# The opening of an attention and MLP kernel: first loads on other queues, shared roots, transposes twice, and a new order list

## The chip, the cores and the metric

The kernel runs on one core of a Trainium2 chip. The metric is the device time of one execution in microseconds; lower is better. The profile shows the engines PE (matrix multiplication; PEld is its weight load), DVE, ACT, POOL and SP. SP, ACT and POOL issue DMA transfers.

## The reference, cut to what matters

```python
def rmsnorm(x, g):
    rms = np.sqrt(np.mean(x * x, axis=-1, keepdims=True) + 1e-06)
    return x / rms * g
q_n, k_n = (rmsnorm(q, g_q), rmsnorm(k, g_k))      # q, k, v: (8, 12, 448, 64)
scores = 1.0 / np.sqrt(64) * np.matmul(q_n, k_n.transpose(0, 1, 3, 2))
attn = softmax(scores)                             # over the last axis
x = np.matmul(attn, v)                             # heads joined: (8, 448, 768)
xn = (x - mu) / np.sqrt(var + 1e-06) * g_ln        # layer norm over 768
out = x + np.maximum(xn @ w_ch1, 0.0) @ w_ch2      # 768 -> 3072 -> 768
```

There are eight batches, each with twelve heads of 448 rows of 64. All inputs and the output are 32-bit.

## The kernel before

Heads are worked on in pairs, six pairs a batch. The 448 rows of a head are 384 main rows, three to a partition, and 64 left rows; the left rows of a pair's two heads lie in the upper and the lower 64 partitions, so each is loaded by a DMA of its own. For each pair the kernel squares, sums and takes the root of queries and keys, scales them, splits the keys into a high and a low 16-bit part, transposes both on PE, multiplies (scores), exponentiates on ACT, multiplies by the values, and then does layer norm and the MLP for the batch.

Batch 0 is cut finely, since nothing is there to overlap with at the start. Its loads are issued by `load_first`. Its work and that of batch 1 stand as names in one list written out by hand, `ORDER`, which `first_attention` walks from front to back. Each name emits the instructions of one step; each engine runs its own instructions strictly in that order and waits by semaphores for the others. The dictionary `ENGINE` says which engine (A for ACT, V for DVE, P for POOL) does a step, where it is not the usual one. After the list, batches 2 to 7 follow a planner that is the same in both kernels.

The names, for key unit u (unit 0 and 1 are pairs 0 and 1, unit 2 and 3 two pairs each):

- `a` square, `d` sum, `h` root (two ACT instructions, Ln and Exp), `n` scale, `j` cast to the high part, `k` subtract for the low part; then `K` transposes a pair's keys on PE into the one bank `tr`, and `C` copies them out (`moved`).
- Queries come in five parts, `0.0`, `0.2`, `1.0`, `2.0`, `2.4`: third of the main rows, and first pair. `qa` square, `qt` sum, `qg` root, `qG` times the weights, `ql` scale, `qm` double (copy the 64 columns beside themselves), `Q` transposes on PE (`turn`), `QC` copies out (`keep`). The tiles `qn` that the parts are scaled into are two buffers in turn.
- `S` scores, `E` exponential, `V` values, `O` division into x, `T` and `A` statistics, `N` and `X` layer norm and its transposes, `XC` their copy, `U` and `R` the first MLP product of batch 0 and its ReLU. `S0.1.0` is query third 0, pair 1, first half. Two banks serve the scores.
- `L4k` loads the keys of unit 4 (batch 1), `z`, `za`, `zb` bring the values to 16 bits on POOL, `W0` and `W1` issue weights from POOL once the keys of unit 4 have landed, `G2` scales the layer norm's weights on POOL, `sp1`, `spm`, `sp2` multiply and spread the two weight vectors g.
- `F23` is 23 filler matmuls of the identity (L824), whose result nobody reads.
- Names without a dot and with a number from 4 on (`c4`, `j4`, `m4`) are the same steps for the units of batch 1.

Of the kernel before, what the change touches and what calls it, by code (L numbers as in the profile page):

```python
# [40 lines left out]
S1.1.1 O0.1 T0.0 qm2.0 qg2.4 E1.1.1 T0.1 S1.2.0 Q2.2 E1.2.0 S1.2.1 E1.2.1 A0 qG2.4 Q2.0 L5k
S1.3.0 V1.1 S1.3.1 ql2.4 E1.3.0 E1.3.1 qm2.4 S1.4.0 E1.4.0 V1.2 N0 S1.4.1 O1.0 QC2.0 X0 S1.5.0
V1.3 QC2.2 E1.4.1 S1.5.1 XC0 E1.5.0 T1.0 Q2.4 V1.4 S2.0.0 E1.5.1 V1.5 S2.0.1 O1.1 QC2.4 L5v
U0.0 E2.0.0 S2.0.2 E2.0.1 S2.1.0 b4 a4 c4 U0.1 E2.0.2 E2.1.0 R0.0 S2.1.1 T1.1 S2.1.2 V2.0 A1 d4
E2.1.1 S2.2.0 i4 N1 E2.1.2 X1 S2.2.1 E2.2.0 j4 V2.1 L5q S2.2.2 E2.2.1 e4 g4 E2.2.2 b5 a5 R0.1
S2.3.0 U0.2 E2.3.0 W2 S2.3.1 S2.3.2 XC1 U1.0 E2.3.2 E2.3.1 S2.4.0 c5 l4 k4 m4 S2.4.1 v4 E2.4.0
i5 E2.4.1 K6 d5 V2.2 S2.4.2 R1.0 C6 S2.5.0 e5 E2.4.2 Q6 V2.3 E2.5.0 D6 S2.5.1 za4 E2.5.1 S2.5.2
E2.5.2 R0.2 V2.4 K7 V2.5 S6.0 S6.1 E6.0 U1.1 O2.0 g5 S6.2 v5 zb4 O2.1 E6.1 U0.3 V6.0 S6.3 j5
E6.2 za5 l5 C7 k5 L6k L6v T2.0 R0.3 U1.2 v6 batch1 R1.1 T2.1 E6.3 za6 L6q S6.4 A2 S6.5 E6.4 zb5
Q7 b6 a6 U1.3 N2 W3 m5 S6.6 V6.1 D7 L7k d6 U1.4 c6 zb6 E6.6 V6.2 E6.5 i6 X2 S7.0 e6 XC2 R1.2  # L50
# [68 lines left out]
class _Fast:  # L119
# [353 lines left out]
    def first_pieces(self):  # L473
# [20 lines left out]

        def root(c):
            nc.scalar.activation(c["rt"], c["ssq"], AFT.Ln, scale=1.0 / D, bias=1e-6)
# [8 lines left out]
        def total(c):
            nc.vector.tensor_reduce(out=c["ssq"], in_=c["sq"], axis=AX.X, op=ALU.add)

        def key_unit(u, p0, m):
# [14 lines left out]
            def low():  # L523
                nc.vector.tensor_tensor(out=c["n"][:, :, 1], in0=k, in1=c["n"][:, :, 0],
                                        op=ALU.subtract)
# [13 lines left out]
        def query_part(ph, p0, p1):  # L539
# [10 lines left out]
            def square():  # L550
                start(c, g, "qn")
                for y, a in zip(src, at):
                    nc.scalar.activation(pair(c["sq"])[:, :, a], y, AFT.Square)
# [15 lines left out]
            def double():  # L569
                _on(nc, f"qm{tag}", "V").tensor_copy(out=c["n"][:, :, 1], in_=c["n"][:, :, 0])  # L570
# [4 lines left out]

            def turn(a, b):
                c["ps", a] = ps = self.ps_m.tile([128, 1024], FP16, tag="mlp", name="psQ")
                y = ps[:, 0:w * (b - a)].rearrange("p (w e s) -> p w e s", e=2, s=w // 2)
                last = n * (b - a) - 1
                for i in range(last + 1):  # L580
                    q, k = divmod(i, n)
                    out = y[:, q, :, 128:192] if k == 2 else y[:, q, k, 0:128]
                    nc.tensor.matmul(out, c["n"][:, n * (a - p0) + i], sh.id16, is_transpose=True,
                                     start=(i == 0), stop=(i == last))

# [724 lines left out]
```

## Time and profile before

| what | value |
|---|---|
| median of three runs | 600.67 us (599.64 to 603.43) |
| profiled execution | 598.46 us, of which the span is 596.8 us |
| PE busy | 580.5 us |
| ACT, DVE, POOL busy | 353.0, 292.7, 189.9 us |
| DMA | 75.25 MB, 126 GB/s on average |

Busy time is summed over the span. The prediction reads the first 60 us in more detail, where PE, DVE and ACT share the work otherwise than later. In rows of groups, the numbers after the first bar are the busy time in us and the mean of one in ns, and after the second the idle time just before and what ended it. In rows of the timeline, the first number is the start and the second the length in us.

### The profile page before, as it was taken

To read this page: it belongs to the slowest core of one execution; us is meant where nothing else is said; L and a number is where in the kernel's file an instruction comes from. 1 tells how busy PE (TensorE), PEld (TensorE's weight loads), DVE (VectorE), ACT (ScalarE), POOL (GpSimd) and SP (SyncE) were. 2 spreads that over 40 slices of the span, in tenths; PEclk is the share of its full clock that TensorE was granted. 3 is DMA by queue.
4 is the path that set the end of the run, shared out by engine and by line. 5 is a ranking of instruction groups with operands and counts; after the bars stand their busy time and mean duration, and the time that the engine had idled before them with its cause. 6 is when DMAs were issued, how large, how long until landed. Compare 5 with 4: busy or idle time off the path is not lost.

```text
span 596.8 us, 12445 instructions
## 1 busy us (share of the span) xinstructions
PE 580.5 (97%) x4989; PEld 361.9 (61%) x4989; DVE 292.7 (49%) x638; ACT 353.0 (59%) x671; POOL 189.9 (32%) x254
## 2 busy tenths in 40 slices
PE   5899999999999999999999999999999999999997
PEld 4889976545565666555566666654566666654565
DVE  6899778444455256724256255724256322440011
ACT  5987784379752897358843598538755387114300
POOL 3769330044650555132541345423512000000000
PEclk9999999999999999999999999999999999999999
DMA  8999998546975776946956496839723320040011
GB/s 268 209 249 203 220 240 186 118 147 106 153 156 134 137 128 128 171 131 73 154 134 140 76 142 145 184 110 124 135 61 88 82 63 1 27 106 1 1 53 57
DMA packets 130225, 75.25 MB, mean 126 GB/s; under 512 B 96468, under 2 KB 120356, under 8 KB 130164
## 3 DMA queue, kind: packets, MB, share of 16 engines
q1 hardware_dynamic: 113636, 44.92, 37.8%
q0 software_dynamic: 16128, 29.27, 23.2%
q8 instruction: 40, 0.66, 0.5%
q10 hardware_dynamic: 400, 0.23, 0.1%
q14 instruction: 21, 0.17, 0.1%
HBM read 52.30 MB, written 11.01 MB: 106 GB/s over the span
## 4 chain that ended last, share of the span: by engine, by line
PE 89%; DMA 4%; SPq 2%; ACT 1%; DVE 1%; POOL 1%; issue 1%; ACTq 0%; POOLq 0%
PE psC L1032 36%; PE psH L998 32%; PE psS L385 8%; PE oA L443 5%; PE psU L695 3%; DMA qkv<-in_v_dram 2%; PE oB L445 2%; PE psS L391 1%; SPq L172 1%; DMA w<-in_k_dram 1%; DMA hT<-in_k_dram 1%; SPq L164 0%; PE tr L353 0%; PE tr L336 0%; POOL gln L832 0%
## 5 line engine op out<-in xcount | busy, mean ns | idle before, releaser
L1032 PE MATMUL psC<-w,hT 128*128 128x384 f16 (+1 forms) x1368 | 235.5, 323 | 0.0
L998 PE MATMUL psH<-xnT,w 128*128 128x512 f16 (+1 forms) x1008 | 217.7, 356 | 0.0
L406 ACT ACTIVATE E<-psS,rr_all 128x448 f16<-128x448 f32 x273 | 171.5, 637 | 60.8 <-PE psS L385 59.3
L1032 PEld LDWEIGHTS <-hT 128*128 128x128 f16 x1368 | 127.1, 98 | 78.4 <-issue 3.9
L1000 ACT ACTIVATE hT<-psH 128x512 f16<-128x512 f32 (+1 forms) x168 | 93.8, 559 | 119.5 <-PE psH L998 117.7
L998 PEld LDWEIGHTS <-w 128*128 128x128 f16 x1008 | 91.1, 98 | 77.7 <-issue 3.0
L385 PE MATMUL psS<-qU,kU 128*128 128x448 f16 x252 | 86.4, 352 | 0.7 <-ACT E L406 0.6
L443 PEld LDWEIGHTS <-E 128*128 128x128 f16 x819 | 56.1, 98 | 35.9 <-issue 1.8
L265 POOL TENSOR_TENSOR qkv<-qkv,gprod 128x896 f32<-128x896 f32 x20 | 41.6, 2081 | 92.4 <-ACT khl L114 71.6
L1039 DVE SCALAR_TENSOR_TENSOR x<-psC,rs_all,x 128x384 f32<-128x384 f32 x48 | 29.3, 616 | 80.7 <-PE psC L1032 80.3
L443 PE MATMUL oA<-v,E 128*128 128x65 f16 x756 | 58.1, 193 | 0.1
L164 POOL DMA_DIRECT2D qkv<-in_k_dram x14 | 11.2, 798 | 122.8 <-ACT E L406 68.2
L456 DVE RECIPROCAL rec_all<-oA 128x6 f32<-128x6 f32 x42 | 8.2, 196 | 83.3 <-PE oA L443 82.8
L445 PE MATMUL oB<-v,E 128*128 128x65 f16 x252 | 45.3, 193 | 0.1
L257 DVE TENSOR_REDUCE ssq<-khl 128x14 f32<-128x896 f32 x21 | 22.7, 1081 | 45.6 <-ACT khl L114 45.5
L385 PEld LDWEIGHTS <-kU 128*128 128x128 f16 x252 | 24.3, 98 | 16.8
L257 DVE TENSOR_REDUCE ssq<-qn 128x14 f32<-128x896 f32 x21 | 22.8, 1084 | 22.1 <-ACT qn L114 22.1
L89 DVE SCALAR_TENSOR_TENSOR qn<-qkv,rr_all 128x256 f16<-128x256 f32 (+2 forms) x71 | 25.3, 416 | 17.0 <-ACT rr_all L261 16.9
L695 PE MATMUL psU<-xnT,w 128*128 128x128 f16 x432 | 27.1, 219 | 0.0
L445 PEld LDWEIGHTS <-E 128*128 128x128 f16 x273 | 26.3, 96 | 0.2 <-DVE xl L463 0.2
L695 PEld LDWEIGHTS <-w 128*128 128x128 f16 x432 | 25.2, 98 | 1.5 <-issue 0.4
L458 DVE TENSOR_TENSOR x<-oA,rec_all 128x384 f32<-128x384 f32 x42 | 23.4, 558 | 1.3
(158 smaller groups left out, 599.5 us busy)
## 6 DMA issues: line engine op xcount, KB each, us to landing
out_dram<-x SPq DMA_DIRECT2D x20, 384.0 KB, 2.5
qkv<-in_v_dram POOLq DMA_DIRECT2D x15, 384.0 KB, 7.2
qkv<-in_k_dram POOLq DMA_DIRECT2D x14, 384.0 KB, 3.9
qkv<-in_q_dram POOLq DMA_DIRECT2D x14, 384.0 KB, 5.4
w<-in_moe_w_ch_dram POOLq DMA_DIRECT2D x3, 1536.0 KB, 12.8
w<-in_moe_w_ch_dram POOLq DMA_DIRECT2D x2, 2304.0 KB, 20.9
qkv<-in_q_dram SPq DMA_DIRECT2D x7, 384.0 KB, 9.7
qkv<-in_v_dram SPq DMA_DIRECT2D x6, 384.0 KB, 8.1
```

Of the source, the lines that this page charges most:

```text
L89: nc.vector.scalar_tensor_tensor(out=out, in0=x, scalar=8.0, in1=r.unsqueeze(2).broadcast_to([x.shape[0], g, D]), op0=ALU.mult, op1=ALU.mult)
L257: nc.vector.tensor_reduce(out=c["ssq"][:, n], in_=c["sq", n], axis=AX.X, op=ALU.add)
L265: _on(nc, f"i{u}", "P").tensor_tensor(out=self.loads[u][1], in0=self.loads[u][1], in1=sh.gprod.unsqueeze(1).broadcast_to([128, g, D]), op= ...
L385: nc.tensor.matmul(ps[0][:, 0:S], c["main"][:, ts(i, 128)], c["q"][:, ts(h, S)], start=True, stop=True)
L406: self.nc.scalar.activation(out=o, in_=c.pop(("ps", i))[:, 0:S], func=AFT.Exp, scale=self.units[u][3][:, g:g + 1], bias=EXP_BIAS)
L443: nc.tensor.matmul(oA[:, t, cs], E[:, ts(t, 128)], rhs, start=(i == 0 and t == 0), stop=(i == 6 and t == 2))
L445: nc.tensor.matmul(oB[:, cs], E[:, 320:448], rhs, start=(i == 0), stop=(i == 6))
L695: nc.tensor.matmul(ps[:, ts(f, 128)], sh.w1[:, dc, ts(4 * k + f, 128)], self.xnT[:, dc, ts(t, 128)], start=(f == 0 and dc == 0), stop=(f = ...
L998: nc.tensor.matmul(ps[:, 0:N], sh.w1[:, dc, ts(f, 128)], xnT[:, dc, 0:N], start=(dc == 0), stop=(dc == NDC - 1))
L1000: nc.scalar.activation(out=hT[:, f, 0:N], in_=ps[:, 0:N], func=AFT.Relu)
L1032: nc.tensor.matmul(self.psC[:, 0:g[1]], self.hT[:, f, ts(t, 128)], sh.w2[:, h, f, c:c + g[1]], start=(f == 0), stop=(f == NFF - 1))
L1039: self.nc.vector.scalar_tensor_tensor(out=x, in0=self.sums.pop((b, t, g[0]))[:, 0:g[1]], scalar=self.rs[:, b, t:t + 1], in1=x, op0=ALU.mul ...
```

## The change

- The second left row of the first pair's keys is issued by SP, as its second DMA, instead of by ACT. The two weight vectors g are issued by ACT instead of by SP. The first query transfer comes after the second pair's keys, the identity is built after all of these.
- Roots are taken for two parts at once, where `ROOTS` says so: `h1` for key unit 1 and query part 0.0, `h2` for key unit 2 and part 0.2, `h3` for key unit 3 and part 1.0; `hq` and `hr` are the roots of the last two parts. The sums of both parts lie in one tile.
- Parts 0.0, 0.2 and 1.0 (`TWICE`) are not doubled before the transposes. Each group of 64 columns is transposed twice instead, into the upper and the lower 64 partitions.
- `ENGINE` and `ORDER` are new. Among others, n0 and qG0.0 go to POOL, j0 and QC0.2 to ACT, C2 and qG2.0 to DVE, and there are 93 fillers instead of 133. The whole of the list is reordered; the first lines are shown, and further on `qa2.4` now stands ahead of `E0.3.0` and `Q1.0`, where it stood behind both, and behind `E0.4.0`.

```diff
--- before.py
+++ after.py
@@ -25,43 +25,45 @@
 PAIR_UNIT = [(u, w) for u, (_, _, m) in enumerate(UNITS) for w in range(m)]
 UNIT_PAIR = [PAIR_UNIT.index((u, 0)) for u in range(len(UNITS))]
 EXP_BIAS = -4.0
-ENGINE = dict(x.split(":") for x in """ j0:P C1:A C2:A C3:A qG0.0:V qm0.0:P QC0.0:A qG1.0:V
-qm2.0:P qm2.4:P QC2.4:A R0.1:V XC1:A R1.0:V R2.0:V R2.3:V R2.4:V R2.5:V a4:P j4:P m4:P a5:V
-j5:P m5:P j6:P m6:P a7:V""".split())
+ENGINE = dict(x.split(":") for x in """ n0:P C1:A C3:A QC0.0:A QC0.2:A qG1.0:V qG2.0:V qm2.0:P
+qm2.4:P QC2.4:A R0.3:V R1.2:V R1.4:V R2.0:V R2.2:V a4:P c4:P j4:P j5:P m5:P j6:P m6:P c7:P j7:P
+m7:P c8:P""".split())
+ROOTS = {"h0": (("k0", 7),), "h1": (("k1", 7), ("q0.0", 4)), "h2": (("k2", 14), ("q0.2", 8)),
+         "h3": (("k3", 14), ("q1.0", 12)), "hq": (("q2.0", 12),), "hr": (("q2.4", 6),)}
+TWICE = ("0.0", "0.2", "1.0")
 Q_PARTS = ((0, 0, 2), (0, 2, 6), (1, 0, 6), (2, 0, 4), (2, 4, 6))
 
 ORDER = """
-G L4k a0 qa0.0 d0 sp1 qt0.0 h0 a1 n0 d1 j0 h1 spm sp2 k0 F23 K0 n1 qG0.0 qg0.0 ql0.0 C0 L4q
-qm0.0 j1 k1 a2 qa0.2 F6 Q0.0 QC0.0 qa1.0 d2 K1 h2 C1 qG0.2 qt0.2 S0.0.0 S0.0.1 z0 qt1.0 za0 z2
-qg0.2 a3 n2 ql0.2 d3 za2 qm0.2 E0.0.1 j2 F42 S0.1.0 zb0 F24 Q0.2 E0.1.0 S0.1.1 k2 qg1.0 K2 h3
-qa2.0 W0 C2 qG1.0 QC0.2 E0.0.0 F16 K3 S0.2.0 n3 E0.1.1 S0.2.1 ql1.0 j3 V0.0 qm1.0 V0.1 k3
-E0.2.1 F10 Q1.0 C3 W1 qt2.0 G2 F8 S0.3.0 L4v E0.2.0 K4 zb2 E0.3.0 S0.3.1 qg2.0 Q1.3 C4 F4
-S0.4.0 K5 z3 QC1.3 E0.3.1 V0.2 S0.4.1 E0.4.0 za3 zb3 qa2.4 C5 QC1.0 qG2.0 V0.3 E0.4.1 S0.5.0
-E0.5.0 O0.0 S0.5.1 S1.0.0 V0.4 E0.5.1 E1.0.0 ql2.0 S1.0.1 S1.1.0 E1.0.1 V0.5 qt2.4 E1.1.0 V1.0
...
+a0 G L4k d0 sp1 h0 spm n0 a1 sp2 d1 qa0.0 qt0.0 j0 qG0.0 h1 k0 F15 K0 n1 j1 ql0.0 Q0.0 k1 a2 C0
+d2 QC0.0 qa0.2 F2 K1 S0.0.0 a3 qG0.2 qt0.2 qa1.0 d3 S0.0.1 h2 E0.0.1 z0 qt1.0 n2 E0.0.0 C1 za0
+F49 S0.1.0 ql0.2 S0.1.1 zb0 h3 j2 qG1.0 Q0.2 k2 E0.1.0 n3 F11 K2 E0.1.1 C2 L4q qa2.0 V0.0 QC0.2
+j3 W0 F11 K3 C3 S0.2.0 W1 E0.2.0 ql1.0 S0.2.1 z2 z3 k3 Q1.3 qt2.0 F5 K4 C4 E0.2.1 S0.3.0 S0.3.1
+qa2.4 E0.3.0 qt2.4 Q1.0 S0.4.0 hq QC1.0 E0.3.1 K5 za2 E0.4.0 L4v S0.4.1 C5 za3 qG2.0 zb2 zb3
+V0.1 S0.5.0 E0.4.1 V0.2 S0.5.1 E0.5.0 V0.3 E0.5.1 ql2.0 S1.0.0 E1.0.0 V0.4 O0.0 G2 S1.0.1 L5k
+E1.0.1 V0.5 S1.1.0 S1.1.1 QC1.3 E1.1.0 O0.1 V1.0 E1.1.1 T0.0 S1.2.0 qm2.0 L5v qG2.4 Q2.2 T0.1
+b4 a4 hr E1.2.0 S1.2.1 Q2.0 S1.3.0 A0 E1.2.1 V1.1 E1.3.0 S1.3.1 V1.2 S1.4.0 E1.3.1 QC2.0 E1.4.0
...
 """.split()
 DMA_UNIT = 8
 IN_W2 = 4
@@ -182,13 +184,14 @@
         key = lambda eng, p: self.load_main(eng, 1, tk[:, p, 0:6], 0, 2 * p, 2)
         main = lambda n, t, p, m: self.load_main(nc.sync, n, t[:, 6 * p:6 * p + 6 * m], 0, 2 * p, 2 * m)
         key(nc.sync, 0)
-        self.load_left(nc.scalar, 1, tk[:, 0:1, 6], 0, 0, 2)
-        main(0, tq, 0, 2)
+        for e, eng in enumerate((nc.scalar, nc.sync)):
+            eng.dma_start(tk[64 * e:64 * e + 64, 0, 6], self.k[0, e, 384:448])
         self.load_left(nc.gpsimd, 1, tk[:, 1:NPAIR, 6], 0, 2, 2 * NPAIR - 2)
-        make_identity(nc, self.sh.id16)
         key(nc.sync, 1)
         for n in range(2):
-            nc.sync.dma_start(self.sh.gg[:, n], self.gs[n].unsqueeze(0))
+            nc.scalar.dma_start(self.sh.gg[:, n], self.gs[n].unsqueeze(0))
+        main(0, tq, 0, 2)
+        make_identity(nc, self.sh.id16)
         key(nc.sync, 2)
         key(nc.sync, 3)
         main(0, tq, 2, 4)
@@ -492,12 +495,27 @@
                 ("ssq", "ssq", dict(bufs=4)), ("rt", "rt", dict(bufs=4)), ("rq", "rr_all", dict(bufs=6)))]
         ops = {}
 
-        def root(c):
-            nc.scalar.activation(c["rt"], c["ssq"], AFT.Ln, scale=1.0 / D, bias=1e-6)
-            nc.scalar.activation(c["r"], c["rt"], AFT.Exp, scale=-0.5)
-
-        def start(c, g, tag):
-            c["ssq"], c["rt"], c["r"] = (y[:, 0:g] for y in sums())
+        place, wide_of, tiles = {}, {}, {}
+        for name, parts in ROOTS.items():
+            at = 0
+            for part, g in parts:
+                place[part] = name, slice(at, at + g)
+                at += g
+            wide_of[name] = at
+
+        def root(name):
+            ssq, rt, r = (y[:, 0:wide_of[name]] for y in tiles[name])
+            nc.scalar.activation(rt, ssq, AFT.Ln, scale=1.0 / D, bias=1e-6)
+            nc.scalar.activation(r, rt, AFT.Exp, scale=-0.5)
+
+        for name in ROOTS:
+            ops[name] = lambda name=name: root(name)
+
+        def start(c, part, g, tag):
+            name, cols = place[part]
+            if name not in tiles:
+                tiles[name] = sums()
+            c["ssq"], c["rt"], c["r"] = (y[:, cols] for y in tiles[name])
             c["n"] = self.p_n.tile([128, 14, 2, D], FP16, tag=tag, name=tag)[:, 0:g]
             c["sq"] = c["n"].rearrange("p g e d -> p (g e d)").bitcast(FP32).rearrange(
                 "p (g d) -> p g d", d=D)
@@ -510,7 +528,7 @@
             k = tk[:, p0:p0 + m].rearrange("p w g d -> p (w g) d")
 
             def square():
-                start(c, g, "khl")
+                start(c, f"k{u}", g, "khl")
                 _square(nc, _on(nc, f"a{u}", "A"), c["sq"], k)
 
             def scale():
@@ -524,8 +542,7 @@
                 nc.vector.tensor_tensor(out=c["n"][:, :, 1], in0=k, in1=c["n"][:, :, 0],
                                         op=ALU.subtract)
 
-            ops.update({f"a{u}": square, f"d{u}": lambda: total(c), f"h{u}": lambda: root(c),
-                        f"n{u}": scale, f"j{u}": high, f"k{u}": low})
+            ops.update({f"a{u}": square, f"d{u}": lambda: total(c), f"n{u}": scale, f"j{u}": high, f"k{u}": low})
             for p in range(p0, p0 + m):
                 ops[f"K{p}"] = lambda p=p: self.keys_turned(
                     c["n"], [7 * (p - p0) + i for i in range(7)])
@@ -548,7 +565,7 @@
                 at.append(slice(2, 3))
 
             def square():
-                start(c, g, "qn")
+                start(c, f"q{tag}", g, "qn")
                 for y, a in zip(src, at):
                     nc.scalar.activation(pair(c["sq"])[:, :, a], y, AFT.Square)
 
@@ -570,7 +587,7 @@
                 _on(nc, f"qm{tag}", "V").tensor_copy(out=c["n"][:, :, 1], in_=c["n"][:, :, 0])
 
             ops.update({f"qa{tag}": square, f"qG{tag}": weight, f"qt{tag}": lambda: total(c),
-                        f"qg{tag}": lambda: root(c), f"ql{tag}": scale, f"qm{tag}": double})
+                        f"ql{tag}": scale, f"qm{tag}": double})
             w = 384 if ph == 2 else 256
 
             def turn(a, b):
@@ -580,8 +597,14 @@
                 for i in range(last + 1):
                     q, k = divmod(i, n)
                     out = y[:, q, :, 128:192] if k == 2 else y[:, q, k, 0:128]
-                    nc.tensor.matmul(out, c["n"][:, n * (a - p0) + i], sh.id16, is_transpose=True,
-                                     start=(i == 0), stop=(i == last))
+                    x = c["n"][:, n * (a - p0) + i]
+                    if tag in TWICE:
+                        for z in range(2):
+                            nc.tensor.matmul(out[64 * z:64 * z + 64], x[:, 0], sh.id16,
+                                             is_transpose=True, start=(i == 0), stop=(i == last))
+                    else:
+                        nc.tensor.matmul(out, x, sh.id16, is_transpose=True, start=(i == 0),
+                                         stop=(i == last))
 
             def keep(a, b):
                 if ph < 2:
```

More of the change, by code (lines that the diff above doesn't have):

```diff
@@ L39 @@
-S0.4.0 K5 z3 QC1.3 E0.3.1 V0.2 S0.4.1 E0.4.0 za3 zb3 qa2.4 C5 QC1.0 qG2.0 V0.3 E0.4.1 S0.5.0
-E0.5.0 O0.0 S0.5.1 S1.0.0 V0.4 E0.5.1 E1.0.0 ql2.0 S1.0.1 S1.1.0 E1.0.1 V0.5 qt2.4 E1.1.0 V1.0
[L41 to L50, printed above, removed]
@@ new lines @@
+T1.1 S2.1.2 E2.1.2 QC2.4 V2.0 S2.2.0 S2.2.1 E2.2.1 U0.0 S2.2.2 e4 E2.2.0 S2.3.0 A1 g4 V2.1
+E2.2.2 E2.3.0 S2.3.1 E2.3.1 N1 l4 X1 j4 S2.3.2 V2.2 E2.3.2 S2.4.0 R0.0 E2.4.0 XC1 V2.3 m4
+S2.4.1 k4 Q6 D6 S2.4.2 E2.4.1 S2.5.0 E2.4.2 U1.0 K6 E2.5.0 S2.5.1 O2.0 C6 L6k S2.5.2 b5 a5
+E2.5.1 V2.4 E2.5.2 T2.0 W2 K7 d5 V2.5 R1.0 v4 S6.0 O2.1 c5 E6.0 S6.1 U1.1 E6.1 S6.2 S6.3 L6v
+U1.2 E6.3 S6.4 i5 e5 v5 E6.2 S6.5 C7 Q7 g5 T2.1 E6.5 za4 zb4 U0.1 j5 E6.4 R1.1 k5 za5 S6.6 D7
+L6q A2 zb5 S7.0 l5 U0.2 b6 a6 V6.0 N2 E6.6 L7k E7.0 S7.1 V6.1 X2 R1.2 XC2 W3 V6.2 V6.3 L7q m5
@@ new lines @@
+K11 S10.1 V9.5 k7 V9.6 v8 C11 E10.0 E10.1 b8 a8 O9 U1.4 S10.2 S10.3 E10.3 R1.4 R2.5 E10.2
+H0.0.0 i8 S10.4 V10.0 H0.0.1 E10.4 V10.1 S10.5 E10.5 U1.5 za8 m7 V10.2 c8 d8 L9k L9q S10.6 Q12
+R1.5 V10.3 j8 H0.0.2 T7 H0.0.3 e8 V10.4 H1.0.0 g8 E10.6 V10.5 E11.6 S11.0 S11.1 V10.6 k8 E11.1
+R l8 L9v D12 H1.0.1 K12 S11.2 zb8 H1.0.2 O10 E11.0 C12 E11.2 S11.3 H1.0.3 V11.0 E11.3 J0.0 L10k
+T9 V11.1 J1.0 V11.2 V11.3 S11.4 E11.4 H2.0.0 S11.5 H2.0.1 E11.5 V11.4 V11.5 S12.0 V11.6 E12.0
+O11 H2.0.2 S12.1 T11 S12.2 H2.0.3 E12.2 H0.1.0 E12.1 S12.3 x8 Y.A Y.N2 H0.1.1 H0.1.2 Y.N0
@@ L65 @@
+H0.1.3 Y.R L10v L10q Y.X0 Y.N1 H1.1.0 E12.3 Y.X1 H1.1.1 J0.1 Y.N3 m8 S12.4 Y.X2 H1.1.2 P0.1
+Y.X3 H1.1.3 J1.1 H2.1.0 H2.1.1 J2.0 S12.5 P1.1 P2.0 y8 H2.1.2 H2.1.3 E12.5 J2.1 P2.1 E12.4 M
 """.split()
```

22 lines of the change are left out of this document (8 added, 14 removed).

## The prediction

> **What bounds the kernel now.** I read the page first, then the stretches, then PE's waits.
>
> ```profile
> span 596.8 us, 12445 instructions
> PE 580.5 (97%) x4989; PEld 361.9 (61%) x4989; DVE 292.7 (49%) x638; ACT 353.0 (59%) x671; POOL 189.9 (32%) x254
> ```
>
> PE is busy 580.5 of 596.8 us, so at most 16.3 us of open idle time is there to win, plus whatever of PE's busy time is filler (L824). The stretches (us; then busy time of PE, PEld, DVE, ACT, POOL; granted clock; DMA) tell where:
>
> ```profile
> 7.00:13.00 6.00, 5.78 (x50) 5.37 (x51) 5.45 (x11) 3.98 (x11) 1.43 (x3) 1.00 1.02 316
> 13.00:25.00 12.00, 10.93 (x188) 10.30 (x187) 11.96 (x16) 11.23 (x25) 7.83 (x10) 1.00 0.89 229
> 25.00:37.00 12.00, 10.04 (x182) 8.89 (x180) 10.35 (x23) 10.11 (x25) 9.75 (x13) 1.00 1.12 220
> 37.00:60.00 23.00, 22.52 (x401) 21.48 (x399) 21.53 (x36) 19.17 (x39) 18.61 (x20) 1.00 1.06 227
> ```
>
> From 13 to 25 us DVE is busy 11.96 of 12 us and ACT 11.23: they set the pace, and PE pads with fillers. From 37 us PE is full (22.52 of 23). So the change, which touches the opening list, works on about 37 us. What PE waited for, and the fillers:
>
> ```profile
> PE psG L744 <- DVE gprod L741: 6.9, 1, 6.9
> PE tr L350 <- DVE kU L343: 1.2, 2, 0.7
> L824 PE MATMUL psW<-id x133: 218/219/314, 7.5 to 25.2; 128*128 128x128 f16 x133
> ```
>
> 6.9 us pass before PE's first matmul, and 133 fillers run between 7.5 and 25.2 us. The opening in the timeline (start, length, engine):
>
> ```profile
> 1.59 0.46 SPq L164 DMA_DIRECT2D qkv<-in_q_dram  x1
> 1.60 1.53 POOL L172 DMA_DIRECT2D hT<-in_k_dram  x2 [0.92 <-POOLq L1294]
> 3.60 0.20 ACT L753 ACTIVATE warm<-ones 128x1 f32<-128x1 f32 x1
> 5.49 0.58 ACT L114 ACTIVATE khl<-hT 128x448 f32<-128x448 f32 x1 [1.69 <-DMA hT<-in_k_dram]
> 6.10 0.62 DVE L506 TENSOR_REDUCE ssq<-khl 128x7 f32<-128x448 f32 x1 [2.89 <-ACT khl L114]
> 7.50 2.37 PEld L824 LDWEIGHTS <-id 128*128 128x128 f16 x23
> 8.51 0.63 DVE L524 TENSOR_TENSOR khl<-hT,khl 128x448 f16<-128x448 f32 x1
> 9.93 0.31 PE L333 MATMUL tr<-id,khl 128*128 128x128 f16 x1
> 12.97 0.55 PE L639 MATMUL psS<-qU,kT 128*128 128x128 f16 x6
> 13.41 2.39 PEld L824 LDWEIGHTS <-id 128*128 128x128 f16 x42
> 16.48 0.38 PE L639 MATMUL psS<-qU,kT 128*128 128x128 f16 x4 [0.50 <-ACT E L650]
> ```
>
> ACT's first square waits 1.69 us for the keys' left rows. The first key operand is done at 8.51 + 0.63 = 9.14, yet its transposes start at 9.93: the 23 fillers ahead of them run until then, at 2.37/23 = 103 ns each. The 42 later ones take 2.39/42 = 57 ns: PE works at half its later rate until about 13 us, though the granted clock stands at 1.00 in every stretch.
>
> **The left row on SP, g on ACT.** The row that ended that wait, in the chain that ended last, and the landings by issue:
>
> ```profile
> 1.67 3.71 DMA hT<-in_k_dram
> hT<-in_k_dram ACTq DMA_DIRECT2D x2, 16.0 KB, 3.2
> hT<-in_k_dram POOLq DMA_DIRECT2D x2, 80.0 KB, 3.9
> ```
>
> ACT's second left row is issued at 1.67 and lands 3.71 us later, at 5.38. The median of ACT's two is 3.2, so the first took about 2.7. In the changed kernel the second row goes out on SP at about 1.59, ahead of the query transfer that stands there now. Bounds: 2.7 us (landing 4.3) and 3.71 us (landing 5.3, nothing won). I take 4.3, since nothing but the first key transfer is then ahead of it on its queue. The cost: SP has three issues of some 0.4 us to 0.5 us in another order and one fewer in all; ACT issues one left row and two g instead of two left rows, and this ends before the activation at 3.60 as now. The first query transfer goes out some 1 us later, but its square now stands behind the second key square anyway.
>
> The Trainium skill ("Trainium Kernel Development and Optimization", Key Constraints) speaks against this edit: queues of SP, ACT and POOL share the same 16 DMA engines, and issuing from several of them saves only the sequencer's issue time. By it, 1.67 - 1.59 = 0.1 us would be won, the start below would fall away, and the sum would be about -0.4 instead of -0.8. The trace bears on it with two ACT issues of the same size that differ by 1 us, so place and moment do count here; it decides nothing more.
>
> **The first chain in the new list.** Durations that it needs, by group (mean ns behind the bar):
>
> ```profile
> L557 POOL TENSOR_TENSOR qkv<-qkv,gprod 128x512 f32<-128x512 f32 x2 | 2.5, 1269 | 1.6 <-ACT qn L553 1.5
> L517 DVE TENSOR_TENSOR hT<-hT,rr_all 128x448 f32<-128x448 f32 x2 | 1.2, 622 | 0.1
> L106 ACT ACTIVATE khl<-hT 128x448 f16<-128x448 f32 x1 | 0.6, 577 | 0.5 <-DVE hT L517 0.5
> L496 ACT ACTIVATE rt<-ssq x9: 189/208/212, 6.8 to 31.3; 128x7 f32<-128x7 f32 x2, 128x14 f32<-128x14 f32 x2, 128x12 f32<-128x12 f32 x2, 128x4 f32<-128x4 f32 x1
> ```
>
> Square 4.35 to 4.9, sum 0.62 to 5.55, root two instructions of 0.21 to 6.05. The scaling n0 moves from DVE (0.62) to POOL, where no instruction of 448 wide stands in the trace; 512 wide take 1.27, so 1.1 by proportion (bounds 0.62 and 1.27), to 7.2. ACT meanwhile squares the second pair (POOL's second left row, about 2.4 + 3.9 = 6.3) and the first query part, then casts (0.58) from 7.3 to 7.9. DVE subtracts to 8.6 and K0's transposes start at 8.6 instead of 9.93. Ahead of them stand 15 fillers, 15 x 0.103 = 1.5 us, over by about 7.7: the block of today is gone. Then n1 0.62, cast 0.58, subtraction 0.63 and the copy C0 0.66 end at 11.1; K1 (7 x 0.103) ends at 11.8, and the first scores start there instead of 12.97: **1.2 us earlier**. ACT then has a3, a square, a root, two exponentials and C1 before the second pair's scores: about 15.8 instead of 16.48, so 0.6 is left. The 49 fillers in between cost 49 x 0.057 = 2.8 us and end before that, if the rate has risen by then.
>
> **Roots of two parts, transposes twice, engines swapped.** Rows for these:
>
> ```profile
> 11.32 0.63 PE L583 MATMUL psQ<-id,qn 128*128 128x128 f16 x4
> 18.04 0.61 PE L583 MATMUL psQ<-id,qn 128*128 128x128 f16 x8
> L570 POOL COPY qn<-qn 128x256 f16<-128x256 f16 x1 | 0.4, 398 | 2.1 <-DVE qn L564 2.1
> L570 DVE COPY qn<-qn x2: 279/320/361, 17.3 to 22.0; 128x512 f16<-128x512 f16 x1, 128x768 f16<-128x768 f16 x1
> L731 DVE COPY qU<-psQ 128x1024 f16<-128x1024 f16 x1 | 0.7, 678 | 0.0
> L731 DVE COPY kT<-tr 128x960 f16<-128x960 f16 x1 | 0.7, 658 | 0.4 <-PE tr L336 0.4
> L729 ACT COPY kT<-tr 128x960 f16<-128x960 f16 x3 | 2.9, 953 | 0.0
> ```
>
> Nine root pairs become six: 3 x 2 x 0.21 = 1.3 us less on ACT, against later starts, since the first part of each pair waits for the other's sum. Doublings of three parts go (0.40 on POOL; 0.28 and 0.36 on DVE); 4 + 8 + 12 = 24 transposes are added. Eight now span 0.61 us and 16 would need 8 x 0.057 = 0.46 more; the first four come in the slow time, 4 x 0.103 = 0.41. Each just about pays for its doubling on its own chain: I count 0, between -0.3 and +0.5 in all. (A transpose of 64 rows does not stand in the trace; bounds half and all of a full one's 57 ns.) On DVE n0 (0.62), qG0.0, the doublings (0.64) and QC0.2 (0.68) go, C2 (0.66) and later qG2.0 come; on ACT C2 (0.95) goes, j0 (0.58) and QC0.2 (about 1.0 by the 960 row) come, which with the roots is -0.7. In DVE's full stretch this is -0.64 - 0.68 + 0.66 = -0.7, between 0 and the -1.3 with n0.
>
> Where does that go? Into a new wait. In the new order the last part's square qa2.4 stands ahead of E0.3.0 on ACT, and waits for PE, whose 12 transposes of Q1.0 still read the buffer it will write; in the old order this square has no wait. Behind it on ACT stand E0.3.0, then the fifth pair's scores, which need its bank. And POOL's weight transfers stretch DVE:
>
> ```profile
> 17.47 1.08 DVE L524 TENSOR_TENSOR khl<-hT,khl 128x896 f16<-128x896 f32 x1
> 21.96 1.72 POOL L905 DMA_DIRECT2D w<-in_moe_w_ch_dram  x2
> 22.29 1.73 DVE L524 TENSOR_TENSOR khl<-hT,khl 128x896 f16<-128x896 f32 x1
> 23.71 2.30 POOL L832 TENSOR_SCALAR gln<-gln 128x768 f32<-128x768 f32 x1
> 25.50 0.40 PE L639 MATMUL psS<-qU,kU 128*128 128x128 f16 x4
> 27.88 0.37 SPq L164 DMA_DIRECT2D qkv<-in_k_dram  x1
> ```
>
> The same subtraction takes 1.08 us alone and 1.73 while POOL issues the weights, as it will again: W0 and W1 wait for the same keys. So of 1.2 us of lead and 0.7 of DVE I keep **0.4** at the fifth pair's scores (25.50 now), between 0 and 1.9. POOL's 2.30 us scaling of g_ln moves behind the values' copies, so the next unit's loads go out some 2 us before 27.88; I count for it and for earlier key copies **0.4**, nearly the 0.5 of the first L350 wait. After that PE is full, and nothing is won or lost.
>
> The sum: -0.4 - 0.4 + 0 = **-0.8 us**. The profiled execution took 598.46 us (span 596.8 and 1.7 around it), so 597.7; the median of the three runs, 600.67, lies 2.2 above it, and by it I predict 599.9 us.
>
> **Rivals.** (1) The lead and DVE's relief arrive in full: 1.2 + 1.3 + 0.5 = 3.0, so 597.7. For it: 40 fillers fewer, 2.3 us at 57 ns. Against: ACT is full beside DVE (11.23 of 12). (2) Slower: PE's higher rate comes late. PE now waits about 1 us before K0, 0.4 before K1; if the rate rises only after the 49 fillers, these take 49 x 0.103 = 5.0, not 2.8: +2.2 - 0.8 = +1.4, so 602.1. It decides from fillers ending past 15.8. If it came only at 25 us, PE's 10.93 us in 13 to 25 would double, with 12 there: 21.9 - 12 - 0.8 = +9, so 610. Against: gaps before K0 and K1 were there before, if shorter. The Trainium skill ("TensorE: Matmul & The Clock Gate", Part 1: The HAM clock gate) says that PE runs at half rate until a free-running window of about 3.4 us was busy; the trace's 103 and 57 ns agree, and a gap in the wrong window gives this rival. (3) Slower by the square that waits: ahead of its release stand the 8 matmuls of S0.3 and the 12 transposes, 20 x 0.057 = 1.1 us in which ACT stands still, and again if squares of batch 1 meet the like; if DVE's 0.7 and the lead are both gone by then, as at the second pair half of it is, 1.1 less the 0.4 later: +0.7, so 601.4. For it: ACT has 0.77 us to spare in 12. Against: the lead. (4) The change does not do what it says: left row at 5.3, transposes eat the doublings' gain: 600.7.
>
> **How the numbers follow.** Chances: forecast 0.56, rival 1 0.14, rival 2 0.13 (0.05 of it the far end), rival 3 0.10, rival 4 0.07. The range joins rival 1 and rival 2's near end, with half the spread of the three runs shown (599.64 to 603.43), 1.9 us, outside each: 596.0 to 604.0. About 1%, 6.0 us, is what a measurement of this kernel can tell from no change. Faster by that takes 0.05, the part of rival 1 in which the later list brings as much again; slower 0.09: the far end of rival 2, and 0.04 of rival 3, if such stops recur in the long list of batch 1; within 0.86.
>
> **What would show it.** First square near 4.3 rather than 5.49; K0 near 8.6; first scores near 11.8; S0.1 near 15.8; a stop on ACT ahead of L570 near 23 us; fifth pair at about 25.1; POOL's next loads' issue near 25.5; PE full from 38 us. Wrong, if the fillers behind the first scores take 100 ns each, if the first square stays at 5.4, or if PE has new waits after 40 us.

## The result, and the profile after

The changed kernel takes 598.07 us (median of 20 runs, 597.09 to 601.21) against 600.09 (20 runs, 598.43 to 603.43) for the kernel before in the same series. The ratio is 0.9966 with a 95% interval of 0.9952 to 0.9980: 2.0 us less, between 1.2 and 2.9. Forecast were 0.8 us less and a time of 599.9. Sign and class are as forecast; the size is too small.

The profiled execution after took 597.09 us, the shortest of its twenty; the one before took 598.46, among the three shortest of its twenty. The page's first line, PE's waits and the stretches that answer to those of before:

```profile
span 595.4 us, 12406 instructions
...
PE psS L662 <- ACT E L673: 1.4, 2, 1.2
PE tr L353 <- DVE kU L346: 0.8, 1, 0.8
```

```profile
13.00:25.00 12.00, 9.97 (x170) 8.79 (x169) 10.94 (x14) 10.76 (x24) 4.29 (x8) 1.00 0.90 226
25.00:37.00 12.00, 11.01 (x187) 9.42 (x185) 11.48 (x26) 10.91 (x25) 11.22 (x13) 1.00 1.11 219
37.00:60.00 23.00, 22.95 (x398) 21.21 (x398) 21.90 (x37) 20.39 (x40) 15.24 (x19) 1.00 1.10 243
```

DVE is no longer full from 13 to 25 us (10.94, was 11.96). PE does more in the next two stretches: 11.01 instead of 10.04 and 22.95 instead of 22.52. That is 1.4 us of idle time less from 25 to 60, and the span is 1.4 us shorter. The opening after, in the timeline:

```profile
4.03 0.56 ACT L116 ACTIVATE khl<-hT 128x448 f32<-128x448 f32 x1
8.72 0.29 PE L336 MATMUL tr<-id,khl 128*128 128x128 f16 x1 [0.91 <-DVE khl L542]
11.79 0.85 PE L662 MATMUL psS<-qU,kT 128*128 128x128 f16 x6
12.29 0.95 ACT L116 ACTIVATE khl<-hT 128x896 f32<-128x896 f32 x1 [0.63 <-DMA hT<-in_k_dram]
12.54 3.48 PEld L847 LDWEIGHTS <-id 128*128 128x128 f16 x49
15.09 0.96 ACT L752 COPY kT<-tr 128x960 f16<-128x960 f16 x1
16.10 0.51 PE L662 MATMUL psS<-qU,kT 128*128 128x128 f16 x6
16.87 0.64 PE L603 MATMUL psQ<-id,qn 128*64 128x128 f16 x16
21.04 1.09 DVE L542 TENSOR_TENSOR khl<-hT,khl 128x896 f16<-128x896 f32 x1
23.69 0.62 ACT L570 ACTIVATE qn<-qkv 128x256 f32<-128x256 f32 x2 [0.95 <-PE psQ L603]
24.84 0.38 PE L662 MATMUL psS<-qU,kU 128*128 128x128 f16 x4 [1.19 <-ACT E L673]
27.18 0.37 SPq L166 DMA_DIRECT2D qkv<-in_k_dram  x1
```

The first square starts 1.46 us earlier, the first scores 1.18, the second pair's scores 0.38, the fifth pair's 0.66. Late markers show what reaches the end; the last copies on DVE but one, before and after:

```profile
590.72 0.42 DVE L1039 SCALAR_TENSOR_TENSOR xl<-psC,rs_all,xl 128x192 f32<-128x192 f32 x1 [1.36 <-PE psC L1032]
```

```profile
589.86 0.42 DVE L1062 SCALAR_TENSOR_TENSOR xl<-psC,rs_all,xl 128x192 f32<-128x192 f32 x1 [1.36 <-PE psC L1055]
```

0.86 us earlier; the other 0.5 us of the spans' 1.4 lies behind this copy, which the change does not touch.

### The profile page after: what moved, and what is told of

Its sections match the earlier page's. It is cut to its first block, busy times and chain, and to the rows that moved or that the text cites. A ratio compares the mean times of both kernels' runs of the same rounds, so it can differ in the third digit from the quotient of the medians.

```text
span 595.4 us, 12406 instructions
## 1 busy us (share of the span) xinstructions
PE 580.2 (97%) x4973; PEld 360.0 (60%) x4973; DVE 290.0 (49%) x634; ACT 350.9 (59%) x664; POOL 191.5 (32%) x256
## 3 DMA queue, kind: packets, MB, share of 16 engines
HBM read 52.30 MB, written 11.01 MB: 106 GB/s over the span
## 4 chain that ended last, share of the span: by engine, by line
PE 91%; DVE 3%; ACT 2%; DMA 2%; issue 1%; SPq 1%; ACTq 0%
PE psC L1055 36%; PE psH L1021 32%; PE psS L388 8%; PE oA L446 5%; PE psU L718 4%; PE oB L448 2%; PE psS L394 1%; DMA hT<-in_k_dram 1%; SPq L166 1%; PE psS L662 1%; PE tr L339 1%; DMA xnT<-xn 1%; DVE qn L581 0%; ACT khl L116 0%; PE tr L356 0%
## 5 line engine op out<-in xcount | busy, mean ns | idle before, releaser
L718 PEld LDWEIGHTS <-w 128*128 128x128 f16 x432 | 25.1, 98 | 1.4 <-issue 0.5
```

Source lines behind the costliest of these rows:

```text
L718: nc.tensor.matmul(ps[:, ts(f, 128)], sh.w1[:, dc, ts(4 * k + f, 128)], self.xnT[:, dc, ts(t, 128)], start=(f == 0 and dc == 0), stop=(f = ...
```

## The experiments

Each ratio is to the kernel before, timed in the same series on the same chip. 0.001 is 0.6 us.

**left_back: the first loads as before, all else changed.**

```
-        for e, eng in enumerate((nc.scalar, nc.sync)):
-            eng.dma_start(tk[64 * e:64 * e + 64, 0, 6], self.k[0, e, 384:448])
+        self.load_left(nc.scalar, 1, tk[:, 0:1, 6], 0, 0, 2)
+        main(0, tq, 0, 2)
...
```

> The changed kernel with the first loads issued as before: both left rows of the first keys on ACT, g on SP, the first query part ahead of the second key transfer. Theory A (the lead at the first square is worth something at the end): first square back at about 5.4 us, first scores near 13, the fifth pair's scores 0.4 to 0.7 later than 24.84, so about 0.5 us of the gain is lost: ratio to the kernel before 0.9975. Theory B (the landings set the pace): the fourth pair of key transfers lands at 12.0 to 12.2 us whichever way the first row goes, ACT's fourth key square starts at about 12.3 as now, the fifth pair's scores stay within 0.2 of 24.84 and the ratio stays at 0.9966.

Ratio 0.9969 (0.9953 to 0.9985), against 0.9966. Its timeline:

```profile
5.88 0.58 ACT L116 ACTIVATE khl<-hT 128x448 f32<-128x448 f32 x1 [2.08 <-DMA hT<-in_k_dram]
25.80 0.38 PE L661 MATMUL psS<-qU,kU 128*128 128x128 f16 x4 [1.19 <-ACT E L672]
```

In this profile the whole lead is lost (fifth pair 0.96 later, against theory B), yet the timed runs keep nearly all of the gain. Their interval holds the ratios of both theories, 0.9975 and 0.9966, so it does not decide between them. By the medians the old order of the loads costs 0.2 us; with both intervals, more than about 1.5 us is unlikely.

**left_only: the first loads alone, in the list of before.**

```
     def load_first(self):
+        (as in the changed kernel; ORDER, ENGINE and query parts as before)
```

> The kernel before, list and engines untouched, with the changed first loads alone (second left row on SP, g on ACT, first query part behind the second key transfer). Theory A (the row matters by itself): first square at 4.0 to 4.7 instead of 5.49, K0's transposes about 1.1 earlier, the first scores near 12, ratio to the kernel before 0.998 to 0.9985. Theory B (the fourth pair of key transfers, landing at 12 to 13 us in every run so far, sets the pace behind the first scores): first scores near 12, but the scores of the second pair within 0.3 of 16.48 and the ratio 1.000.

Ratio 1.0013 (0.9990 to 1.0036): no gain to be seen. Three rows of its timeline:

```profile
7.25 0.42 ACT L554 ACTIVATE qn<-qkv 128x256 f32<-128x256 f32 x1 [2.06 <-DMA qkv<-in_q_dram]
13.22 0.84 PE L640 MATMUL psS<-qU,kT 128*128 128x128 f16 x6
31.76 0.51 PE L584 MATMUL psQ<-id,qn 128*128 128x128 f16 x6 [1.24 <-POOL qn L571]
```

In the old list the first scores come no earlier (12.97 before), which neither theory had. The first row says why: the first square starts at 4.61 instead of 5.49, but the old list has the first query square next on ACT, and the query transfer now goes out behind the second key transfer. ACT stands 2.06 us for it, and the second key square, behind it, starts at 7.91 instead of 7.10. So this run tests the new loads in a list that is not made for them, not the left row by itself. And PE still stops at 31.76 us for POOL's doubling of the fourth query part: the fifth pair's lead of 0.26 us (25.24) is 0.03 there (31.79 before).

**qg2_pool: the weighting of the fourth query part back on POOL.**

```
-ENGINE = ... qG1.0:V qG2.0:V qm2.0:P
+ENGINE = ... qG1.0:V qm2.0:P
```

> The changed kernel with one entry taken out: the weighting of the fourth query part (qG2.0) runs on POOL again, as in the kernel before, not on DVE. Theory A (part of the gain that the prediction did not count comes from this swap): PE's wait for POOL's doubling (1.1 us at 31.79 in the kernel before, gone now) comes back with 0.8 to 1.5 us, and the ratio rises from 0.9966 to about 0.998 to 0.999. Theory B (that wait was covered by the later list): PE waits elsewhere less by as much, ratio 0.9966.

Ratio 1.0005 (0.9991 to 1.0019): all of the gain is gone, more than expected, and in another place than theory A had it. PE's wait and the stretch that holds it; then the timeline there:

```profile
PE oA L694 <- POOL vl L635: 2.5, 1, 2.5
...
25.00:37.00 12.00, 9.06 (x139) 8.30 (x139) 8.19 (x18) 7.80 (x20) 11.15 (x15) 0.86 1.09 202
```

```profile
17.42 0.50 PE L662 MATMUL psS<-qU,kT 128*128 128x128 f16 x6
30.16 0.54 PE L694 MATMUL oB<-v,E 128*128 128x65 f16 x6
```

In the new list this weighting stands on POOL ahead of the last casts of the values (1.94 us from 27.12 on), and PE waits 2.5 us for them. Behind that wait six products take 0.54 us instead of 0.35, and the granted clock of the stretch is 0.86. This is the longest of the run's twelve executions (603.67 us, median 600.25): the next keys, for which POOL waits ahead of all this, came 0.9 us later than in the changed kernel's profile, and at 119.56 us PE stands another 1.9 us for a transfer. So the profile shows the place of the loss, and only the timed runs its size. This profile also shows the fillers in the way: the copy that the second pair's scores need ends at 16.42, but they start at 17.42, behind the 49 fillers.

**doubled: the first three query parts doubled by a copy, as before.**

```
-TWICE = ("0.0", "0.2", "1.0")
+TWICE = ()
 (qm0.0, qm0.2, qm1.0 behind ql0.0, ql0.2, ql1.0 in ORDER; qm0.0 on POOL)
```

> The changed kernel with the first three query parts doubled by a copy and transposed once, as before (copies of 0.40 us on POOL, 0.28 and 0.36 on DVE), not transposed twice. As predicted on record (each pays for the other): 0, ratio 0.9966. Theory A (16 transposes of 64 rows took 0.64 us, as long as 8 full ones, so the second ones are free and the copies are not): DVE is full again between 13 and 23 us, the fifth pair's scores come 0.3 to 0.7 later than 24.84, ratio 0.9972 to 0.998.

Ratio 0.9995 (0.9980 to 1.0010): the gain is gone, or nearly. Its waits and two rows of its timeline:

```profile
PE psQ L606 <- POOL qn L587: 0.9, 2, 0.5
PE psQ L606 <- DVE qn L587: 0.7, 2, 0.5
...
13.43 0.95 ACT L116 ACTIVATE khl<-hT 128x896 f32<-128x896 f32 x1 [0.99 <-DMA hT<-in_k_dram]
18.34 0.62 PE L606 MATMUL psQ<-id,qn 128*128 128x128 f16 x8 [0.48 <-DVE qn L587]
26.57 0.38 PE L662 MATMUL psS<-qU,kU 128*128 128x128 f16 x4 [1.19 <-ACT E L673]
```

PE now waits for the doublings on POOL and DVE. Eight full transposes take 0.62 us; the changed kernel's 16 of 64 rows take 0.64. So the second transposes cost PE next to nothing, while the copies cost their time: theory A, at more than its price. Of the 1.73 us by which the fifth pair is later, up to 1.14 belong to the fourth key square, which waited longer for its landing (13.43 against 12.29) though its load is the same. This execution, too, is one of the run's longest (601.79 us, median 599.87).

**apart: nine pairs of roots, in the places of the six.**

```
-            nc.scalar.activation(rt, ssq, AFT.Ln, scale=1.0 / D, bias=1e-6)
+            for part, g in ROOTS[name]:
+                ssq, rt, r = (y[:, place[part][1]] for y in tiles[name])
+                nc.scalar.activation(rt, ssq, AFT.Ln, scale=1.0 / D, bias=1e-6)
...
```

> The changed kernel with the shared roots taken apart in place: nine pairs of root instructions on ACT, not six, each at the place of the shared pair. Theory A (ACT sets the pace between 12 and 24 us): three more pairs cost up to 3 x 2 x 0.21 = 1.3 us less overlap, about 0.23 each pair as they follow each other, so 0.5 to 0.7 us at the fifth pair's scores, ratio 0.9975. Theory B (ACT has the time: it stood 0.63 and 0.95 us): the fifth pair within 0.2 of 24.84, ratio 0.9966 to 0.997.

Ratio 0.9993 (0.9978 to 1.0009); the loss is three times what theory A had. Its timeline:

```profile
13.06 0.95 ACT L116 ACTIVATE khl<-hT 128x896 f32<-128x896 f32 x1 [0.81 <-PE psS L667]
17.21 0.51 PE L663 MATMUL psS<-qU,kT 128*128 128x128 f16 x6 [0.45 <-ACT kT L753]
```

The second pair's scores, 1.11 us later, wait for ACT's copy; so ACT's time counts here. But up to 0.77 of the 1.11 us stem from the fourth key square, which starts at 13.06 against 12.29. ACT stood 0.81 us ahead of it, so the pair of roots before it cost nothing; some 0.3 us is left for the pair behind it. Where the timed loss of 1.6 us comes from, these rows do not say.

**no_stop: the new wait on ACT taken away.**

```
-S0.3.1 qa2.4 E0.3.0 qt2.4 Q1.0 S0.4.0 hq QC1.0 E0.3.1 K5 za2 E0.4.0 L4v S0.4.1 C5 za3
+S0.3.1 E0.3.0 Q1.0 S0.4.0 hq QC1.0 E0.3.1 qa2.4 K5 za2 E0.4.0 L4v S0.4.1 C5 qt2.4 za3
```

> The changed kernel with the square of the last query part (qa2.4) behind the two exponentials of the fourth pair on ACT, and its sum behind the copy C5 on DVE, so that ACT no longer stands 0.95 us for the 12 transposes. Theory A (this new wait costs what ACT stands): the fifth pair's scores at about 23.6 to 23.9 instead of 24.84, PE's wait of 1.2 us for the exponential gone or below 0.3, ratio 0.9950 to 0.9958 against 0.9966. Theory B (the next link is as late: DVE's copies and the values): fifth pair earlier, but PE waits 0.5 to 1 us elsewhere before 30 us, ratio 0.9966.

Ratio 0.9992 (0.9975 to 1.0009): worse than the changed kernel. Its timeline and the stretch:

```profile
23.29 0.38 PE L662 MATMUL psS<-qU,kU 128*128 128x128 f16 x4
28.14 0.22 PE L694 MATMUL oA<-vl,E 128*128 128x130 f16 x1 [2.45 <-POOL vl L635]
28.58 0.54 PE L694 MATMUL oB<-v,E 128*128 128x65 f16 x6
...
25.00:37.00 12.00, 9.41 (x140) 8.50 (x140) 9.19 (x20) 7.71 (x18) 10.86 (x13) 0.86 1.09 211
```

The fifth pair's scores are 1.55 us earlier, as theory A had it; then PE runs into the values, the next link, and stands 2.45 us. The slow rate follows. Theory B holds, with a price that it had too low. Not all of the stand is PE's lead: the product that waits starts at 28.14, where it starts at 26.80 in the changed kernel, so the values themselves came 1.3 us later in this execution. POOL's copy that waits for the next keys ended 0.3 later, and its casts took longer (3.93 us in all, not 3.17).

**no_stop_f40: the same, with 40 fillers in that wait.**

```
-E0.4.1 V0.2 S0.5.1
+E0.4.1 F40 V0.2 S0.5.1
```

> no_stop with 40 fillers ahead of the third pair's value products (V0.2), where PE stood 2.5 us for the values. The wait for the values itself stays, it is only filled. Theory A (half the loss is the rate: after a stand of 2.5 us PE works at half rate for 3.4 us): the products behind it at 0.35 us for six instead of 0.54, granted clock 1.00 instead of 0.86 from 25 to 37, the following scores 1.3 to 1.7 earlier than in no_stop, ratio 0.9970 against 0.9992. Theory B (the wait alone counts): ratio 0.9992 or, if the fillers run past the values' landing, higher.

Ratio 0.9975 (0.9961 to 0.9989), on another chip than no_stop. The stretch and the products behind the fillers:

```profile
26.80 2.40 PE L847 MATMUL psW<-id 128*128 128x128 f16 x40
29.65 0.35 PE L694 MATMUL oB<-v,E 128*128 128x65 f16 x6
...
25.00:37.00 12.00, 11.08 (x194) 9.81 (x193) 10.56 (x21) 8.89 (x22) 11.22 (x14) 1.00 1.03 192
```

With the stand filled, the six products take 0.35 us and the granted clock is 1.00. The scores behind them are not earlier than in no_stop, as theory A had it, for this execution's opening is later: its fifth pair's scores start at 24.86 us, not 23.29. Counted from there, the fifth pair's scores of the next query third come after 9.93 us (34.79) instead of 11.05 (34.34). So the filled stand saves about 1.1 us, and the two ratios differ by 1.0, though their intervals overlap. Against the changed kernel's 7.40 us the wait itself is still there.

**early: the second pair's copy and the third root ahead of the fourth key square, 25 fillers.**

```
-d2 QC0.0 qa0.2 F2 K1 S0.0.0 a3 qG0.2 qt0.2 qa1.0 d3 S0.0.1 h2 E0.0.1 z0 qt1.0 n2 E0.0.0 C1 za0 F49
+d2 QC0.0 qa0.2 F2 K1 S0.0.0 C1 qt0.2 h2 a3 qG0.2 qa1.0 d3 S0.0.1 E0.0.1 z0 qt1.0 n2 E0.0.0 za0 F25
```

> The changed kernel with the copy of the second pair's keys (C1) and the root of the third (h2) ahead of the fourth key square on ACT, which waits for a landing at 12.2, and with 25 instead of 49 fillers behind the first scores. Theory A (ACT's and DVE's 0.65 us of waiting for that landing is what holds the opening): the scaling of the third unit's keys starts near 13.2 instead of 15.13, the second pair's scores near 15.2 instead of 16.10, the fifth pair's 0.4 to 0.7 earlier than 24.84, ratio 0.9955 to 0.996. Theory B (the fourth key square and what follows is then later by as much on ACT): fifth pair within 0.2, ratio 0.9966. If the fewer fillers leave PE at its slow rate beyond 17 us, the transposes of the second part take 1.2 us instead of 0.64 and the ratio rises to 0.998.

Ratio 1.0004 (0.9986 to 1.0023), slower than every branch had it. Its timeline and the stretch:

```profile
12.69 2.71 PEld L847 LDWEIGHTS <-id 128*128 128x128 f16 x25
17.99 0.64 PE L603 MATMUL psQ<-id,qn 128*64 128x128 f16 x16 [1.41 <-DVE qn L581]
19.93 0.84 PE L339 MATMUL tr<-id,khl 128*128 128x128 f16 x6
...
13.00:25.00 12.00, 10.08 (x128) 9.28 (x127) 9.80 (x11) 9.63 (x19) 4.93 (x9) 0.86 0.92 223
```

The second pair's scores come 0.59 us earlier (15.51), the fifth pair's 2.25 later (27.09). The fillers run at 108 ns, and PE then stands 1.41 us. The 16 transposes behind the stand take 0.64 us, the full rate, so the slow rate did not last as the third branch had it. But it came back: six transposes at 19.93 us take 0.84 us instead of 0.50, and the granted clock of the stretch is 0.86. Order and fillers were changed at once, so the share of each is open.

**all_twice: the last two query parts transposed twice too.**

```
-TWICE = ("0.0", "0.2", "1.0")
+TWICE = ("0.0", "0.2", "1.0", "2.0", "2.4")
```

> The changed kernel with the last two query parts transposed twice as well: POOL's copies qm2.0 (0.81 us at 29.39) and qm2.4 go, 18 transposes of 64 rows come. Theory A (the second ones are free, as 16 in 0.64 us say, and POOL's later work moves up by 0.8): ratio 0.996. Theory B (nobody waits for POOL there): 0.9966. If a transpose of 64 rows costs a full one's 57 ns, 18 x 0.057 = 1.0 us is lost on a full PE: 0.9983.

Ratio 1.0046 (1.0030 to 1.0063), slower than every theory had it. In its waits stands

```profile
PE tr L1007 <- DVE xn L975: 2.4, 1, 2.4
...
34.26 2.10 DVE L581 TENSOR_TENSOR qn<-qkv,rr_all 128x256 f16<-128x256 f32 x2
36.29 2.82 DVE L975 SCALAR_TENSOR_TENSOR xn<-x,stat,gln 128x768 f16<-128x768 f32 x1
37.00:60.00 23.00, 20.67 (x331) 18.86 (x332) 21.81 (x35) 17.71 (x36) 11.55 (x14) 0.93 1.05 220
```

The transposes are not the cost. With POOL's copies gone, what comes behind them on POOL moves up and meets DVE's work: its squares and a product run from 32.68 to 38.30 us. Beside them DVE's two scalings take 2.10 us instead of 0.62, and the normalized rows 2.82 instead of 1.01. PE waits 2.4 us for these rows, six 65-wide products behind the wait take 0.54 us, and the granted clock falls to 0.93. This profile also has a wait of 1.3 us for the values, ahead of the place of the edit.

**values_first and both: the values' casts ahead of the weight transfers, without and with no_stop.**

```
-C2 L4q qa2.0 V0.0 QC0.2 j3 W0 ... W1 E0.2.0 ql1.0 S0.2.1 z2 z3
+C2 L4q qa2.0 V0.0 QC0.2 j3 z2 za2 zb2 z3 za3 zb3 W0 ... W1 E0.2.0 ql1.0 S0.2.1
```

> The changed kernel with the casts of the values of the third to sixth pair (z2, z3 and their left rows) ahead of the weight transfers W0 and W1 on POOL, which there waits some 7 us for the landing of w at 21.7 to 23.5. Theory A (the values are the next link, a few tenths behind PE, and in executions with later landings PE runs into them): POOL's casts at 16.7 to 20 instead of 24.05 to 27.2, the scaling of g_ln near 24.1 instead of 27.25, no wait of PE for vl, ratio 0.9950 to 0.996 against 0.9966. Theory B (only the square on ACT holds the opening): ratio 0.9966. If POOL's casts stretch DVE's subtractions (1.08 us) as its weight transfers did (1.73), the fifth pair's scores come 0.5 later and the ratio is 0.9975.

> values_first and no_stop together: the last query part's square behind the fourth pair's exponentials, the values' casts ahead of the weight transfers. Theory A (no_stop's lead of 1.5 us at the fifth pair was lost in PE's wait of 2.5 us for the values and in the slow rate that followed it): fifth pair's scores near 23.3, no wait for vl, granted clock 1.00 from 25 to 37, ratio 0.9930 to 0.9945. Theory B (the next link behind the values, DVE or the landings, is as late): ratio 0.995 to 0.9966.

Ratios 1.0008 (0.9993 to 1.0023) and 1.0024 (1.0010 to 1.0039). The timeline of values_first, a cast on POOL and a subtraction on DVE:

```profile
18.43 1.46 POOL L630 CAST v<-qkv 128x768 f16<-128x768 f32 x1 [1.89 <-DMA qkv<-in_v_dram]
19.11 1.71 DVE L542 TENSOR_TENSOR khl<-hT,khl 128x896 f16<-128x896 f32 x1
```

The wait for the values is gone, but beside POOL's casts DVE's subtraction takes 1.71 us instead of 1.08. The third branch of the expectation, the stretched DVE, is what came, at more than its price: the fifth pair's scores start 2.74 us later (27.58), of which up to 1.5 belong to a fourth key square that starts at 13.80. In the run both, the values' wait and the slow rate are gone as theory A had it (granted clock 1.00 from 25 to 37 us), but the fifth pair comes at 25.19, not 23.3: DVE's weighting takes 1.58 us beside the casts instead of 0.95, and the subtractions 1.17. Its ratio lies above every theory's.

**before_again: a second profile of the kernel before.**

> The kernel before, unchanged, looked at a second time: its profiled execution of 598.46 us was among the three shortest of twenty (median 600.09), while the changed kernel moved the last copy on DVE by only 0.87 us in its own profile and the medians by 2.0. Theory A (longer executions of it lose in the opening, where landings come later): the fourth pair of key transfers lands at 12.3 to 13.3 instead of 11.98, the first half of PE's waits lies before 35 us, and the last copy on DVE comes as much after 590.72 as the execution is longer. Theory B (they lose behind the last copy, where 5.5 to 7.5 us passed in the runs so far): the copy stays near 590.7. Ratio 1.000, which also shows how far apart two series of one kernel lie.

Ratio 1.0003 (0.9986 to 1.0020); its profiled execution took 598.76 us. Two rows of PE, and the same late copy on DVE:

```profile
31.48 0.50 PE L583 MATMUL psQ<-id,qn 128*128 128x128 f16 x6
58.40 1.51 PE L695 MATMUL psU<-xnT,w 128*128 128x128 f16 x24 [0.27 <-DMA w<-in_moe_w_ch_dram]
591.52 0.42 DVE L1039 SCALAR_TENSOR_TENSOR xl<-psC,rs_all,xl 128x192 f32<-128x192 f32 x1 [1.36 <-PE psC L1032]
```

The copy is 0.80 us later than in the first profile, and the execution 0.30 longer. So two profiles of one kernel differ by as much as the forecast. Neither theory fits this pair. The opening is late, with the fifth pair's scores at 26.50 us instead of 25.50, but that does not last: the transposes that stood 1.15 us for POOL's doubling in the first profile (31.79) start at 31.48 without a wait, and the MLP products at 56.12 us are 0.65 ahead of the first profile's. Then PE waits for the landing of weights (0.27 us at 58.40) and for ACT (0.34 at 60.71), and the products at 61.72 us are 0.81 behind. So the 0.80 was lost between 58 and 62 us. This execution was a short one too; what long ones do stays open.

## Why the prediction was right, and where its size was off

**The first chain.** First square 4.03 (said: 4.35), K0 8.72 (8.6), first scores 11.79 (11.8, 1.18 us earlier instead of 1.2): the chain held. The row on SP landed in time. By the rule of the Trainium skill ("Trainium Kernel Development and Optimization", Key Constraints) that was weighed there, nearly nothing was to be won. The chain speaks against it, with a first square 1.46 us earlier; the time speaks for it: undoing the new loads costs 0.2 us and hardly more than 1.5 (left_back). left_only does not decide it, since there ACT stands for the queries.

**From the first to the second pair.** Said was 15.8, found 16.10, since the step summed ACT's instructions and left out a landing: the fourth key square waits 0.63 us for its keys, and the second pair's copy behind it ends at 16.05. The 49 fillers took 3.48/49 = 71 ns each, not 57, and ended at the same moment. That is rival 2 in a mild form; in qg2_pool's execution it cost 1.0 us.

**Roots and transposes: the mis-sized term.** Counted at 0, between -0.3 and +0.5. Taken out one at a time, either loses about all of the gain (ratios 0.9993 and 0.9995 against 0.9966, some 1.6 to 1.7 us each), and so does the weighting on DVE (1.0005). They do not add up. Edits that were meant as help lost as much or more (no_stop, early, values_first), so these losses may only mean that the list is fitted closely to its steps; they do not show what each step is worth. No run adds the roots, the transposes or the swaps to the old list. The price of a 64-row transpose was the lower bound, half a full one. The Trainium skill ("TensorEngine Tiling (Array Packing)", Theoretical Speedup) has it: with up to 64 columns, two tiles work side by side, up to twice as fast; 16 in 0.64 us beside 8 in 0.61 agree.

**The stop on ACT.** Right in place and size: 0.95 us at 23.69 (said: 1.1 near 23). The fifth pair was at 24.84 instead of 25.1; the stretched subtraction that was kept in the sum did not come (1.09 us, with the weight transfers behind it). Rival 3's price was real; no_stop shows why undoing it brings nothing: the values on POOL are the next link.

**The later 0.4.** PE's waits for kU went from 1.2 us (two) to 0.8 (one), as said, but not for the reason given. The next loads went out at 27.18, not 25.5: SP waited 5.2 us for the values' casts, whose place behind the weight transfers the step overlooked. And the second profile of the kernel before has only one such wait too (0.7), so its first one comes and goes without the change. That this 0.4 came out is luck.

```profile
SPq L166 <- POOL vl L635: 5.2, 1, 5.2
```

And a wait was left out of the sum altogether: in the kernel before PE stops for POOL's doubling, and this stop swallows leads, as left_only's row at 31.76 us shows. The second profile shows the same from the other side: 1.00 us late at the fifth pair, it is not late at 31.48. After, the weighting runs on DVE, and this wait is gone from the list. That the swap alone removed it is not shown, since qg2_pool's profile stops earlier, at the values.

```profile
PE psQ L583 <- POOL qn L570: 1.1, 1, 1.1
```

**The size.** In the profiles the late copy moved by 0.86 us, close to the 0.8; in the timed runs the gain is 2.0 (1.2 to 2.9). Both profiles are of short executions (598.46 beside a median of 600.09 before, 597.09 beside 598.07 after), so the 0.86 compares one short execution with another; against the second profile of the kernel before the copy moved by 1.66. That second one lost its time from 58 us on, around a wait for weights that the changed kernel's list does not have. How often longer executions lose time there or in the waits above stays open: no long one of the kernel before was profiled. Open too is how the gain is shared between roots, transposes and weighting, and whether fewer fillers alone would help.

No version tried beats the changed kernel: left_back at 0.9969 and no_stop_f40 at 0.9975 come nearest, within its interval.

## What to carry to other kernels

When an opening is a chain over five engines, read the whole list of PE's waits, the small ones too: a lead made early lives only to the next of them, which has to go too. Price a stand of PE by what follows it as well: filling a stand of 2.45 us here saved about 1.1 us. And weigh one profile against the spread of the times before taking a difference of 1 us from it.
